# Token mixer behind adaLN linear attention on one core: fp32r sums for modulation and phi(k), u in contiguous parts, a last step cut in two

## The chip, the cores and the metric

The kernel runs on one core of a Trainium2 chip. The metric is the device time of one execution in microseconds (us). The engines of the core are named as in the profile: PE is TensorE (matmuls, with PEld for its weight loads), DVE is VectorE, ACT is ScalarE, POOL is GpSimd, and SP issues most DMAs. An engine executes its instructions in the order in which the program gives them to it, and waits where an operand is not there yet.

## The reference

Two residual blocks act on x, 2048 tokens by 448 channels, under one conditioning vector c. All values are fp32.

```python
mod = (_silu(c) @ w_mod).reshape(c.shape[0], 6, 1, -1)        # w_mod: 448 x 2688
sa, ca, ga, sb, cb, gb = (mod[:, j] for j in range(6))

h = _layernorm(x, axis=-1) * (1 + ca) + sa
q, k, v = split_heads(h @ wqkv)                               # 16 heads of 28
phi = lambda t: jnp.where(t > 0, t + 1, jnp.exp(t)) + 1e-6
pq, pk = phi(q), phi(k)
kv = einsum("bhsd,bhse->bhde", pk, v)
z = einsum("bhsd->bhd", pk)                                   # phi(k)'s sum over the tokens
o = einsum("bhqd,bhde->bhqe", pq, kv) / (einsum("bhqd,bhd->bhq", pq, z)[..., None] + 1e-6)
x = x + ga * (merge_heads(o) @ wo)

h = _layernorm(x, axis=-1) * (1 + cb) + sb
h = _layernorm(h, axis=-1)
u = gelu(einsum("bsd,sf->bdf", h, w1) + b1)                   # w1: 2048 x 1792, over the tokens
y = einsum("bdf,fs->bds", u, w2) + b2                         # w2: 1792 x 2048
x = x + gb * y.transpose(0, 2, 1)
```

## The kernel before, in words

**Arithmetic.** Most products run on TensorE in the type fp32r, and an operand that has to keep its accuracy is split into a high part, rounded to fp32r by an ACT copy, and a low part, the rest, made by a VectorE subtraction (`split`, lines 73 to 75). The product of two split operands is three matmuls: high by high, high by low, low by high (`acc3`, lines 708 to 711). Some low parts are made without VectorE: ACT writes the negated high part, and a DMA that GpSimd issues adds the full value to it in memory (`low`, lines 353 to 358; `w_low_dma`, lines 190 to 199). A few small sums use plain fp32 matmuls instead.

**Tiles.** Tokens go in 16 tiles of 128 (`NT`), the hidden dimension of the mixer in 14 tiles of 128 (`NF`). Most temporary tiles are taken from a pool of 76 slots of 2 KB per partition; a new tile waits until the earlier owner of its slot is done. The program fixes the order of the instructions by hand (`manual_schedule`).

**The stages**, in the order in which they run:

1. *Start* (lines 431 to 510). The vectors sa and ca of the modulation, then the first tiles of tokens. A modulation vector j is the sum over the 448 rows of silu(c) times a part of `w_mod`, 112 rows by 448 in each of four tiles. VectorE makes one accumulated tile of the four with the functions `mod_acc` (all at once) or `mod_part` (one tile at a time), and `mod_sum` (lines 168 to 174) adds its 112 rows with an fp32 matmul by a matrix of ones, which also spreads the result over the 128 partitions. `mod_out` copies it out of PSUM.
2. *The phi(k) loop* (lines 514 to 561), t = 3 to 15. TensorE projects k of tile t (`kp`, 11 matmuls), transposes the normalized tile t+1, and adds the outer product of tile t-3 (`a_outer`, `cacc`, 11 matmuls). VectorE and ACT make phi(k) (`a_exp` and `phi_k`, lines 321 to 329: exponential on ACT; minimum with 1 and addition of 1e-6 on VectorE; then the larger of k and 0 added on VectorE), its parts (`a_pk_parts`, lines 373 to 384), the statistics, norm and parts of the tiles ahead (`a_stats`, `a_norm_a`, `a_norm_b`, `a_high`). Phi(k) of most tiles is added to one of two running sums by a DMA of GpSimd (line 383). The vector j = 2 is made in steps 5 to 8 and summed in step 10; the parts of `w_mod` for j = 4 and 3 are loaded in steps 10 and 11.
3. *Closing the attention's sums* (lines 564 to 606). The last outer products; phi(k)'s sum `zp` over partitions by two fp32 matmuls with ones (lines 574 to 576); the vectors j = 4 and j = 3, `mod_acc` on VectorE and `mod_sum` on TensorE; the product with the v weights (`kvb`). Projections of q that were put off (`late`) fill in.
4. *The attention output and the mixer's norms* (lines 730 to 789, called stage B in this document), i = 0 to 20. Per step TensorE transposes the scaled phi(q) (`tq`), makes the attention's output of the tile before (`op`), and from step 5 on adds the product of a normalized tile and the first 512 columns of w1 (`up`). VectorE, ACT and GpSimd make the denominators (`den`, `pn`), the residual and two norms in a chain. The normalized tile's low part (`b_low2`, h2l) is made just before the next tile's scaled phi(q) (`b_scale`, pn). The vector j = 5 is added up in steps 13 to 16 and summed in step 16.
5. *First mixer product* (lines 996 to 1019): u for the other columns, only TensorE in bulk. `finish_u` applies Gelu and the factor gb, and cuts u of each hidden tile into the operands of the second product.
6. *Second mixer product* (lines 1022 to 1040). Token tiles 0 to 9 go through a scheme of seven products for each two-by-two block (`mult7`), where the moving operand is a half of u's columns (224) with its high and low part, 448 columns in all, followed by a matmul of 224 columns. Token tiles 10 to 15 are plain (`mult1`): three matmuls of all 448 columns per hidden tile. The last ten steps of the program's order are plain ones of tile 15. After the last hidden tile, VectorE adds the sum to x and SP stores the tile (`out1`, `store`).

In `finish_u` the tile `uw[f]` (4 x 224 columns) is laid out as left high, left low, right high, right low (lines 818 to 824), so that a seven product reads 448 neighbouring columns and a plain one reads two runs of 224:

```python
w4 = uw[f].rearrange("p (h x d) -> p x h d", h=2, x=2)
split(ufull[f].rearrange("p (h d) -> p h d", h=2), w4[:, 0], w4[:, 1])
```

Of the kernel before, what the change touches and what calls it, by code (L numbers as in the profile page):

```python
# [8 lines left out]
F32 = mybir.dt.float32  # L9
# [19 lines left out]
AHEAD = 8  # L29
LAG = 5  # L30
QS = {0: 2, 4: 2}
WARM = 12
# [10 lines left out]
def block_kernel(ctx: ExitStack, tc: tile.TileContext, x, wqkv, wo, w1, b1, w2, b2, c, wmod, out):  # L43
# [34 lines left out]
    ones = cst.tile([P, P], F32, name="ones")  # L78
    nc.vector.memset(ones, 1.0)
    ident = cst.tile([P, P], F32, name="ident")  # L80
    make_identity(nc, ident)
# [86 lines left out]
    def mod_sum(j, n=4):  # L168
        ps = bank(f"modp{j}")
        todo = [(scb[:, (k - 2) * P:(k - 1) * P], wm[j, k]) for k in range(n, 4)]  # L170
        todo.insert(1, (ones[:G, :], macc.pop(j)))
        for k, (a, b) in enumerate(todo):
            nc.tensor.matmul(ps[:, :D], a, b, start=(k == 0), stop=(k == len(todo) - 1))
        return ps

# [145 lines left out]
    def a_exp(t, ps):  # L321
        eks[t] = slot(f"ek{t}")
        nc.scalar.activation(eks[t], ps, AF.Exp)

    def phi_k(t, ps, new):
        dst, e = new(f"pk{t}"), eks.pop(t)
        nc.vector.tensor_scalar(e, e, 1.0, 1e-6, op0=ALU.min, op1=ALU.add)
        nc.vector.scalar_tensor_tensor(dst, ps, 0.0, e, op0=ALU.max, op1=ALU.add)
        return dst
# [145 lines left out]
    a_norm_b(2)  # L475
    w_low_dma(0, 1)
    a_stats(3)
# [36 lines left out]
    for t in range(3, NT):  # L514
# [6 lines left out]
        if t == 10:  # L521
            mp = mod_sum(2)
        if t + 1 < NT:
# [21 lines left out]
        if 5 <= t < 9:  # L545
            mod_part(2, t - 5)
        if t in (10, 11):
            load_mod(14 - t)
# [22 lines left out]
    nc.vector.tensor_add(pksum[2], pksum[2], pksum[1])  # L571
    a_q(late.pop(0))
    mod_acc(4)
    zp = bank("zp")
    for i, pk in enumerate((pksum[0], pksum[2])):
        nc.tensor.matmul(zp[:, :D], ones, pk, start=(i == 0), stop=(i == 1))
# [14 lines left out]
    split_to(6)  # L591
    mp = mod_sum(4)
    mod_acc(3)
    kvb = bank("kvb")
# [8 lines left out]
    mod_out(4, mp)  # L603
    mp = mod_sum(3)
    load_to(PRE + MID + 3)
# [125 lines left out]
    for i in range(NT + LAG):  # L731
        if i == NT - 4:
            load_mod(5)
        if NT - 3 <= i <= NT:
            mod_part(5, i - NT + 3)
        if i < NT:
            b_transpose(i)
# [5 lines left out]
        t = i - LAG  # L743
        mp = mod_sum(5) if i == NT else None
        if t >= 0:
# [58 lines left out]
    def u_parts(r, name, src):  # L804
        w = slot(f"u{name}_{r}", dt=F32R)
        split(src, w[:, :HD], w[:, HD:])
        uops[name, r] = w

    def finish_u(f, ps):
# [72 lines left out]
    def mult7(q, m):  # L882
        a, b, k, _ = PRODS[m]
        opens = m in (0, 1, 3)
        if opens:
            acc2[q, k] = bank(f"y{q}_{k}")
        ps = acc2[q, k]
        closes = m in (1, 5, 6)
        cut = hilo.pop((q, m))
        for r in range(PAIRS):  # L890
            (h, l), i = cut[r // 4], r % 4
            w = uops[b, r]
            s = slice(i * P, (i + 1) * P)
            nc.tensor.matmul(ps[:, :D], h[:, s], w, start=opens and r == 0, stop=False, skip_group_check=True)  # L894
            nc.tensor.matmul(ps[:, :HD], l[:, s], w[:, :HD], start=False, stop=closes and r == PAIRS - 1,  # L895
                             skip_group_check=True)
# [45 lines left out]
    def mult1(t, n, f):  # L942
# [3 lines left out]
        hi, lo = hilo.pop((t, n, f))  # L946
        w4 = uw[f].rearrange("p (h x d) -> p x h d", h=2, x=2)
# [74 lines left out]
    for n, (kind, p) in enumerate(order):  # L1022
# [44 lines left out]
```

## Time and profile before

| What | Before |
|---|---|
| Time, median of 3 runs | 456.86 us (456.37 to 457.12) |
| Time of the profiled execution | 457.06 us |
| Its span (first to last instruction) | 455.3 us |
| Granted TensorE clock, mean | 1.00 |
| DMA packets | 60550, 61.85 MB, mean 136 GB/s |
| phi(k) loop, projections of t = 3 to 15 | about 32.6 to 99.1 us |
| Stage B with the first 512 columns of u | about 124 to 235 us |
| First mixer product, the rest | about 235 to 323 us |
| Second mixer product | about 323 to 452 us |

The page of a profile gives for each engine its busy time, share of the span and number of instructions. Groups of instructions show line, engine, operation, output and inputs, shapes, count, then total busy time and the mean of one in ns, then the idle time of the engine before them and what ended it. The chain of waits follows the execution back from its last instruction, at each step to what released it. Matmuls overlap in a pipeline: the duration shown for one (0.36 us for 448 columns) holds its latency, and the distance between the starts of neighbours is what it costs.

### The profile page before, as it was taken

The numbers are of one execution on the slowest core, as the hardware profiler recorded it, in microseconds if no ns is written. First come the engines' busy times: TensorE is split into PE (matmuls) and PEld (weight loads), VectorE is DVE, ScalarE is ACT, GpSimd is POOL, SyncE is SP. The second block draws the span as 40 slices with busy tenths as digits, with TensorE's granted clock in tenths as the row PEclk, the third lists the DMA queues.
The fourth block names the chain that finished last, engine by engine and source line by source line (L and its number), as shares of the span: only waits on it lengthen the run. The fifth ranks groups of instructions, "written<-read, shape, count | busy, mean of one in ns | idle before, by whom it ended". The sixth has DMA issues, their size and how long they took to land.

```text
span 455.3 us, 7265 instructions
## 1 busy us (share of the span) xinstructions
PE 448.9 (99%) x2378; PEld 409.9 (90%) x2378; DVE 356.6 (78%) x781; ACT 241.7 (53%) x538; POOL 91.6 (20%) x163
## 2 busy tenths in 40 slices
PE   8999999999999999999999999999999999999996
PEld 7589998988799999988999999999999999999995
DVE  4798897887899798896559676639696977798982
ACT  1649766644466576676675445236546262535350
POOL 2124676620014355554300000000000000000000
PEclk9999999999999999999999999999999999999999
DMA  7979999994200003322307553317960583528312
GB/s 220 283 186 168 170 175 225 229 219 141 71 1 2 23 24 88 74 50 48 116 22 228 171 187 113 115 40 235 281 185 23 186 231 120 170 96 254 112 57 97
DMA packets 60550, 61.85 MB, mean 136 GB/s; under 512 B 9248, under 2 KB 53856, under 8 KB 60512
## 3 DMA queue, kind: packets, MB, share of 16 engines
q1 hardware_dynamic: 54752, 52.45, 38.5%
q0 software_dynamic: 5760, 8.95, 12.0%
q8 instruction: 18, 0.29, 0.3%
q14 instruction: 20, 0.16, 0.1%
HBM read 45.09 MB, written 7.34 MB: 115 GB/s over the span
## 4 chain that ended last, share of the span: by engine, by line
PE 80%; POOL 4%; ACT 4%; DVE 4%; DMA 3%; issue 3%; SPq 1%; POOLq 0%; DVEq 0%
PE y L894 11%; PE up L711 8%; PE up L710 8%; PE up L709 8%; PE qp L316 7%; PE y L895 6%; PE cacc L398 5%; PE kp L316 5%; PE yp L709 4%; PE yp L711 4%; PE yp L710 4%; PE op L658 4%; DMA pkl<-pk 2%; DMA wm<-in_w_mod_dram 1%; ACT y L700 1%
## 5 line engine op out<-in xcount | busy, mean ns | idle before, releaser
L711 PE MATMUL up<-h2h,pl 128*128 128x448 f32 x224 | 81.3, 363 | 0.0
L710 PE MATMUL up<-h2l,ph 128*128 128x448 f32 x224 | 81.2, 362 | 0.0
L709 PE MATMUL up<-h2h,ph 128*128 128x448 f32 x224 | 81.1, 362 | 0.0
L75 DVE TENSOR_TENSOR pl<-pr,ph 128x512 fp32r<-128x512 f32 (+1 forms) x60 | 36.4, 616 | 12.3 <-ACT ph L74 7.9
L710 PEld LDWEIGHTS up<-h2l,ph 128*128 128x128 f32 x224 | 42.1, 188 | 3.3 <-issue 0.2
L709 PEld LDWEIGHTS up<-h2h,ph 128*128 128x128 f32 x224 | 41.9, 187 | 3.1 <-issue 0.2
L711 PEld LDWEIGHTS up<-h2h,pl 128*128 128x128 f32 x224 | 42.0, 188 | 2.4
L74 ACT ACTIVATE ph<-pr 128x512 fp32r<-128x512 f32 (+1 forms) x60 | 32.8, 567 | 15.9 <-PE up L710 11.1
L900 ACT ACTIVATE cc<-y 128x448 f32<-128x448 f32 x15 | 8.2, 546 | 55.4 <-PE y L895 38.6
L709 PE MATMUL yp<-uw,qw 128*128 128x448 f32 x84 | 31.2, 371 | 0.0
L710 PE MATMUL yp<-uw,qw 128*128 128x448 f32 x84 | 30.6, 365 | 0.0
L711 PE MATMUL yp<-uw,qw 128*128 128x448 f32 x84 | 30.6, 365 | 0.0
L398 PE MATMUL cacc<-pkh,xh 128*128 128x448 f32 x64 | 24.6, 385 | 0.0
L658 PE MATMUL op<-wph,pth 112*128 112x448 f32 x64 | 24.5, 383 | 0.0
L74 ACT ACTIVATE qw<-q 128x256 fp32r<-128x256 f32 (+1 forms) x56 | 18.9, 353 | 9.0 <-DMA q<-in_B_w_dram 8.5
L398 PE MATMUL cacc<-pkl,xh 128*128 128x448 f32 x64 | 23.3, 363 | 0.2 <-DMA pkl<-pk 0.2
L658 PE MATMUL op<-wph,ptl 112*128 112x448 f32 x64 | 23.2, 362 | 0.0
L658 PE MATMUL op<-wpl,pth 112*128 112x448 f32 x64 | 23.2, 362 | 0.0
L316 PE MATMUL kp<-wh,hh 128*128 128x448 f32 x60 | 22.0, 371 | 0.0
L316 PE MATMUL qp<-wh,hh 128*128 128x448 f32 x60 | 21.9, 371 | 0.0
L75 DVE TENSOR_TENSOR qw<-q,qw 128x256 fp32r<-128x256 f32 (+1 forms) x56 | 18.9, 352 | 3.8 <-ACT qw L74 3.8
L316 PE MATMUL kp<-wh,hl 128*128 128x448 f32 x60 | 21.7, 366 | 0.1
(198 smaller groups left out, 1221.0 us busy)
## 6 DMA issues: line engine op xcount, KB each, us to landing
pr<-in_B_w_dram SPq DMA_DIRECT2D x48, 256.0 KB, 3.0
a<-in_B_w_dram SPq DMA_DIRECT2D x20, 256.0 KB, 5.0
wm<-in_w_mod_dram SPq DMA_DIRECT2D x24, 196.0 KB, 5.0
a<-in_B_w_dram SPq DMA_DIRECT2D x20, 192.0 KB, 4.9
x<-in_A_x_dram SPq DMA_DIRECT2D x16, 224.0 KB, 4.6
xpark<-x SPq DMA_DIRECT2D x16, 224.0 KB, 1.9
q<-in_B_w_dram SPq DMA_DIRECT2D x28, 128.0 KB, 3.3
xb<-xpark SPq DMA_DIRECT2D x16, 224.0 KB, 4.1
```

The costliest lines, as they stand in the source:

```text
L74: nc.scalar.activation(hi, full, AF.Copy)
L75: nc.vector.tensor_sub(lo, full, hi.bitcast(F32))
L316: nc.tensor.matmul(o, a[:, ch * P:(ch + 1) * P], b, start=(n == 0), stop=(n == 10))
L398: nc.tensor.matmul(cacc[ch][:, :D], a[:, s], b, start=(t == 0 and i == 0), stop=(t == NT - 1 and i == len(todo) - 1))
L658: nc.tensor.matmul(opb[t][:, :D], a[:, s], b, start=(n == 0), stop=(n == 11))
L700: nc.scalar.activation(ys[t], ys[t], AF.Identity, bias=nb, scale=rs)
L709: nc.tensor.matmul(ps[:, :D], hi[:, sl], mh, start=first, stop=False)
L710: nc.tensor.matmul(ps[:, :D], hi[:, sl], ml, start=False, stop=False)
L711: nc.tensor.matmul(ps[:, :D], lo[:, sl], mh, start=False, stop=last)
L894: nc.tensor.matmul(ps[:, :D], h[:, s], w, start=opens and r == 0, stop=False, skip_group_check=True)
L895: nc.tensor.matmul(ps[:, :HD], l[:, s], w[:, :HD], start=False, stop=closes and r == PAIRS - 1, skip_group_check=True)
L900: nc.scalar.activation(cop[q, name], acc2[q, k][:, :D], AF.Copy)
```

## The change

It has seven parts.

1. *Modulation vectors j = 2 to 5*: the accumulated tile is split (`mod_split`) and summed by two fp32r matmuls with a matrix of ones in fp32r (`mod_sum2`) instead of one fp32 matmul. Vectors 0 and 1 stay as they are.
2. *Additions for j = 4 and j = 3*: one tile of `w_mod` at a time, in steps 11 to 14 (j = 4) and, two and two, in step 15 and just after the loop (j = 3), instead of `mod_acc` in the stage after the loop.
3. *phi(k)'s sum*: both running sums are added on VectorE, the result is split and summed by two fp32r matmuls, now behind the last outer product.
4. *phi(k)*: ACT also makes a Relu of k, and VectorE does one operation, min(exp, 1) + Relu, instead of two. The constant 1e-6 is added while the parts are made, and to z when `zb` is copied (2048 times 1e-6).
5. The low part of one q weight tile (`w_low(0, 1)`) by VectorE instead of ACT and GpSimd's DMA; and in stage B `b_scale` ahead of `b_low2`.
6. *u in contiguous parts*: `uw[f]` holds all 448 high columns, then all 448 low columns. A plain product reads one run of 448; the seven products that read u itself (b11, b21, b22) read two runs of 224. The operands of the other four (t1 to t4) stay contiguous.
7. *The last three hidden tiles of token tile 15*: the sum so far is closed and added to x; the nine remaining matmuls are done for columns 0 to 335, then for columns 336 to 447, each with its own PSUM bank, addition and store.

```diff
+LAST, CUT = 3, 336
+MOD_AT = {11: [(4, 0)], 12: [(4, 1)], 13: [(4, 2)], 14: [(4, 3)], 15: [(3, 0), (3, 1)]}
...
+    ones_r = cst.tile([P, P], F32R, name="ones_r")
+    nc.scalar.activation(ones_r, ones, AF.Copy)
...
+    def mod_split(j):
+        acc = macc.pop(j)
+        macc[j] = (moving(slot, f"mh{j}", parts=G), moving(slot, f"ml{j}", parts=G))
+        split(acc, *macc[j])
+
+    def mod_sum2(j):
+        ps = bank(f"modp{j}")
+        hi, lo = macc.pop(j)
+        nc.tensor.matmul(ps[:, :D], ones_r[:G, :], hi, start=True, stop=False)
+        nc.tensor.matmul(ps[:, :D], ones_r[:G, :], lo, start=False, stop=True)
         return ps
...
     def a_exp(t, ps):
-        eks[t] = slot(f"ek{t}")
-        nc.scalar.activation(eks[t], ps, AF.Exp)
+        eks[t] = (slot(f"ek{t}"), slot(f"rk{t}"))
+        nc.scalar.activation(eks[t][0], ps, AF.Exp)
+        nc.scalar.activation(eks[t][1], ps, AF.Relu)
+
     def phi_k(t, ps, new):
-        dst, e = new(f"pk{t}"), eks.pop(t)
-        nc.vector.tensor_scalar(e, e, 1.0, 1e-6, op0=ALU.min, op1=ALU.add)
-        nc.vector.scalar_tensor_tensor(dst, ps, 0.0, e, op0=ALU.max, op1=ALU.add)
+        dst, (e, r) = new(f"pk{t}"), eks.pop(t)
+        nc.vector.scalar_tensor_tensor(dst, e, 1.0, r, op0=ALU.min, op1=ALU.add)
         return dst
...
-        nc.scalar.activation(hi, pk, AF.Copy)
-        low(t, lo, pk, hi)
+        nc.scalar.activation(hi, pk, AF.Copy, bias=1e-6)
+        if t in DVE_LOW:
+            nc.vector.scalar_tensor_tensor(lo, pk, 1e-6, hi.bitcast(F32), op0=ALU.add, op1=ALU.subtract)
+        else:
+            nc.scalar.activation(lo, hi.bitcast(F32), AF.Copy, scale=-1.0, bias=1e-6)
+            nc.gpsimd.dma_start(lo, pk, accum_op=ALU.add)
...
-    w_low_dma(0, 1)
+    w_low(0, 1)
...
         if t == 10:
-            mp = mod_sum(2)
+            mp = mod_sum2(2)
...
+        if t == 9:
+            mod_split(2)
+        for j, i in MOD_AT.get(t, ()):
+            mod_part(j, i)
...
+    for i in (2, 3):
+        mod_part(3, i)
     split_to(2)
     nc.vector.tensor_add(pksum[2], pksum[2], pksum14[0])
     nc.vector.tensor_add(pksum[2], pksum[2], pksum[1])
     a_q(late.pop(0))
-    mod_acc(4)
+    nc.vector.tensor_add(pksum[2], pksum[2], pksum[0])
+    zs = (moving(slot, "zh"), moving(slot, "zl"))
+    split(pksum[2], *zs)
+    a_outer(NT - 1)
     zp = bank("zp")
-    for i, pk in enumerate((pksum[0], pksum[2])):
-        nc.tensor.matmul(zp[:, :D], ones, pk, start=(i == 0), stop=(i == 1))
-    a_outer(NT - 1)
+    for i, pk in enumerate(zs):
+        nc.tensor.matmul(zp[:, :D], ones_r, pk, start=(i == 0), stop=(i == 1))
+    mod_split(4)
+    mod_split(3)
     load_to(14)
     split_to(4)
     zb = tslot("zb")
-    nc.scalar.activation(zb, zp[:, :D], AF.Copy)
+    nc.scalar.activation(zb, zp[:, :D], AF.Copy, bias=S * 1e-6)
...
-    mp = mod_sum(4)
-    mod_acc(3)
+    mp = mod_sum2(4)
...
-    mp = mod_sum(3)
+    mp = mod_sum2(3)
...
+        if i == NT:
+            mod_split(5)
...
-        mp = mod_sum(5) if i == NT else None
+        mp = mod_sum2(5) if i == NT else None
...
+        if scale:
+            b_scale(i + 1)
         if norm2:
             b_low2(i - 4)
-        if scale:
-            b_scale(i + 1)
...
-            w4 = uw[f].rearrange("p (h x d) -> p x h d", h=2, x=2)
-            split(ufull[f].rearrange("p (h d) -> p h d", h=2), w4[:, 0], w4[:, 1])
+            split(ufull[f], uw[f][:, :D], uw[f][:, D:])
+            w = uw[f].rearrange("p (x d) -> p x d", x=2)
+            left, right = ((w[:, :, h:h + HD], w[:, 0, h:h + HD]) for h in (0, HD))
             if f % 2:
-                uops["b21", r], uops["b22", r] = uw[f][:, :D], uw[f][:, D:]
+                uops["b21", r], uops["b22", r] = left, right
             else:
-                uops["b11", r] = uw[f][:, :D]
+                uops["b11", r] = left
...
-            acc3(acc2[t + i], hi, lo, slice(i * P, (i + 1) * P), w4[:, 0], w4[:, 1], f == 0, f == NF - 1)
+            acc3(acc2[t + i], hi, lo, slice(i * P, (i + 1) * P), uw[f][:, :D], uw[f][:, D:], f == 0,
+                 f == NF - 1 - (LAST if t == NT - 1 else 0))
+
+    def mult_last(t):
+        nc.vector.tensor_add(X[t], acc2[t][:, :D], X[t])
+        for c0, c1 in ((0, CUT), (CUT, D)):
+            ps = bank(f"yl{c0}")[:, :c1 - c0]
+            n = 0
+            for f in range(NF - LAST, NF):
+                wh, wl = hilo[t, 1, f]
+                a, b = uw[f][:, c0:c1], uw[f][:, D + c0:D + c1]
+                for w, m in ((wh, a), (wh, b), (wl, a)):
+                    nc.tensor.matmul(ps, w, m, start=n == 0, stop=n == 3 * LAST - 1)
+                    n += 1
+            x = X[t][:, c0:c1]
+            nc.vector.tensor_add(x, ps, x)
+            nc.sync.dma_start(of[t * P:(t + 1) * P, c0:c1], x)
...
-        (mult7 if kind == "s" else mult1)(*p)
-        (out7 if kind == "s" else out1)(*p)
+        if n < len(order) - LAST:
+            (mult7 if kind == "s" else mult1)(*p)
+            (out7 if kind == "s" else out1)(*p)
+    mult_last(NT - 1)
```

More of the change, by code (lines that the diff above doesn't have):

```diff
@@ L173, in mod_sum @@
             nc.tensor.matmul(ps[:, :D], a, b, start=(k == 0), stop=(k == len(todo) - 1))
+        return ps
+    def mod_split(j):
[7 more added lines that the diff above has]
+        nc.tensor.matmul(ps[:, :D], ones_r[:G, :], lo, start=False, stop=True)
         return ps
@@ L806, in u_parts @@
         split(src, w[:, :HD], w[:, HD:])
-        uops[name, r] = w
+        uops[name, r] = (w, w[:, :HD])
     def finish_u(f, ps):
@@ L891, in mult7 @@
             (h, l), i = cut[r // 4], r % 4
-            w = uops[b, r]
+            w, wh = uops[b, r]
             s = slice(i * P, (i + 1) * P)
             nc.tensor.matmul(ps[:, :D], h[:, s], w, start=opens and r == 0, stop=False, skip_group_check=True)
-            nc.tensor.matmul(ps[:, :HD], l[:, s], w[:, :HD], start=False, stop=closes and r == PAIRS - 1,
+            nc.tensor.matmul(ps[:, :HD], l[:, s], wh, start=False, stop=closes and r == PAIRS - 1,
                              skip_group_check=True)
@@ L946, in mult1 @@
         hi, lo = hilo.pop((t, n, f))
-        w4 = uw[f].rearrange("p (h x d) -> p x h d", h=2, x=2)
         for i in range(n):
-            acc3(acc2[t + i], hi, lo, slice(i * P, (i + 1) * P), w4[:, 0], w4[:, 1], f == 0, f == NF - 1)
+            acc3(acc2[t + i], hi, lo, slice(i * P, (i + 1) * P), uw[f][:, :D], uw[f][:, D:], f == 0,
[14 more added lines that the diff above has]
+            nc.sync.dma_start(of[t * P:(t + 1) * P, c0:c1], x)
     def out1(t, n, f):
```

## The prediction

> **What bounds the kernel now.** The page of the profile comes first: the engines' busy time and, further down, the shares of the chain that ended last.
>
> ```profile
> PE 448.9 (99%) x2378; PEld 409.9 (90%) x2378; DVE 356.6 (78%) x781; ACT 241.7 (53%) x538; POOL 91.6 (20%) x163
> ...
> PE 80%; POOL 4%; ACT 4%; DVE 4%; DMA 3%; issue 3%; SPq 1%; POOLq 0%; DVEq 0%
> ```
>
> TensorE works from end to end. Its busy figure overlaps neighbouring matmuls, so I price a matmul by the distance between starts. The chain of waits in order of time (start, duration, what) gives such distances; these rows surround the edits.
>
> ```profile
> 92.34 2.08 PE kp L316 x9
> ...
> 105.87 2.20 PE qp L316 x11
> 108.07 1.50 PE zp L576 x4
> 109.57 2.21 PE cacc L398 x11
> 111.79 2.21 PE qp L316 x11
> 113.99 0.75 PE modp L173 x2
> 114.75 3.15 PE kvb L598 x32
> 117.89 0.77 PE modp L173 x2
> ...
> 214.64 0.75 PE modp L173 x2
> ```
>
> An fp32r matmul of 448 columns takes 2.20/11 = 0.200 us; an fp32 one counts as two instructions and takes 1.50/2 = 0.75 us. From 105.87 to 118.66 the chain is TensorE's without a gap. In two stretches it also runs through other engines: around 64 to 92 us, in the phi(k) loop, and 159 to 207 us, in what I call stage B. The timeline (start, duration, engine, line, tiles, wait) shows what TensorE lost there.
>
> ```profile
> 74.18 0.47 PE L398 MATMUL cacc<-pkl,xh 128*128 128x448 f32 x1 [0.24 <-DMA pkl<-pk]
> 195.09 0.37 PE L711 MATMUL up<-h2h,pl 128*128 128x448 f32 x1
> 195.84 0.62 PE L642 MATMUL tq<-ident,pn 128*112 128x128 f32 x4 [0.38 <-DVE pn L631]
> 206.19 0.37 PE L711 MATMUL up<-h2h,pl 128*128 128x448 f32 x1
> 206.78 0.62 PE L642 MATMUL tq<-ident,pn 128*112 128x128 f32 x4 [0.23 <-DVE pn L631]
> ```
>
> The next start is due 0.20 after a matmul's; 195.09 to 195.84 is 0.75 and 206.19 to 206.78 is 0.59, so TensorE lost 0.55 + 0.39 = 0.94 us waiting for pn. The rest is nearly a sum of matmuls, and the change is priced as that sum.
>
> **zp, phi(k)'s sum.** Two fp32 matmuls (1.50) become two fp32r ones (0.40): **-1.10 us**. Their operand must be split first: three additions of VectorE instead of two, an ACT copy and a subtraction now precede zp. It is also moved behind the last outer product (2.21), so it starts near 105.87 + 2.20 + 2.21 = 110.28. In the old trace the second addition starts at 105.48:
>
> ```profile
> 105.48 0.62 DVE L571 TENSOR_TENSOR pk<-pk,pk 128x448 f32<-128x448 f32 x1
> ```
>
> Four such steps end near 107.9, 2.4 us ahead of zp; without that cover, what exceeds it is a stall. ACT's copy zb now comes near 110.9 and the two copies of cacc queue behind it, so all three end by about 112.5 at 0.54 each (L334 below); kvb, which waits for them, starts at 110.68 + 2.20 + 0.40 = 113.3. Covered, by 0.8 us.
>
> **The modulation vectors j = 2 to 5.** For j = 4, 3 and 5 the sums go from 0.75 + 0.77 + 0.75 to 3 x 0.40: **-1.07 us**. The eight additions for j = 4 and 3 leave VectorE between 106 and 117 us and go to steps 11 to 15 of the phi(k) loop and just behind it. SP had issued w_mod's part 4 long before:
>
> ```profile
> 65.15 2.18 SPq L107 DMA_DIRECT2D wm<-in_w_mod_dram  x4
> ```
>
> Step 11 ends near 88 (below), 20 us later, and part 3 has a similar lead, so I charge no wait for a DMA. For j = 5 a split now stands between the last addition and the matmul:
>
> ```profile
> 211.69 0.63 ACT L226 ACTIVATE pl<-ph 128x512 fp32r<-128x512 f32 x1
> ```
>
> ACT is free at 212.3; a copy and a subtraction of some 0.6 each end near 213.5, the matmul starts at 214.64: hidden by 1.1 us, or by 0.4 if TensorE gains 0.74 on ACT before (below). Behind the waiting subtraction VectorE queues the residual of the next tile, and GpSimd waits for its sum to make the mean. If the cover goes, up to 0.5 is lost.
>
> **The phi(k) loop.** Per step VectorE loses L327 (a minimum and an addition in one), ACT gains a Relu like L334, and steps 11 to 14 gain one addition like L166 (mean ns behind the busy time):
>
> ```profile
> L334 ACT ACTIVATE rq<-qp 128x448 f32<-128x448 f32 x16 | 8.7, 541 | 0.0
> L327 DVE TENSOR_SCALAR ek<-ek 128x448 f32<-128x448 f32 x16 | 6.2, 386 | 1.5 <-ACT ek L323 1.5
> L905 DVE TENSOR_TENSOR xb<-xb,cc 128x224 f32<-128x224 f32 x15 | 5.9, 392 | 0.5
> L166 DVE SCALAR_TENSOR_TENSOR acc<-wm,sc,acc 112x448 f32<-112x448 f32 x6 | 4.1, 679 | 0.0
> ```
>
> Before step 11 VectorE's 0.39 a step is worth nothing where TensorE bounds, and ACT, half busy, has room for 0.54. In steps 11 to 14 VectorE has 0.68 - 0.39 = 0.29 more. Step 11 hides it, step 12 does not:
>
> ```profile
> 87.96 0.69 DVE L283 SCALAR_TENSOR_TENSOR h<-h,rs,mod 128x448 f32<-128x448 f32 x1 [0.44 <-POOL rs L272]
> 91.60 0.68 DVE L75 TENSOR_TENSOR hl<-tp,hh 128x512 fp32r<-128x512 f32 x1
> ```
>
> VectorE idles 0.44 for GpSimd's rs before 87.96, then runs to hl, which ends at 92.28; TensorE's kp goes on at 92.34. So the 0.35 that j = 2 wins at step 10 is waited away here, and VectorE's 0.29 may be added; and the Relu delays ACT's pkl copy, whose DMA came just in time at 74.18. Bounds: -0.35 (all kept) to +0.8 (0.29 and one Relu of 0.54). I take **0.0** for this part, j = 2 included, since the rows show another chain level with TensorE there. One w_low moves from ACT and GpSimd's queue to VectorE, 0.62 against the 0.39 dropped beside it: nothing. The constant ones_r is made at the start, where ACT waits for c.
>
> **b_scale ahead of b_low2.** pn, which ended the stalls, stood behind the subtraction h2l:
>
> ```profile
> 194.10 0.24 DVE L627 RECIPROCAL den<-den 128x16 f32<-128x16 f32 x1
> 194.53 0.62 DVE L706 TENSOR_TENSOR h2l<-y,h2h 128x448 fp32r<-128x448 f32 x1 [0.19 <-ACT h2h L703]
> 195.08 0.62 DVE L631 SCALAR_TENSOR_TENSOR pn<-pq,den 128x448 f32<-128x448 f32 x1
> ```
>
> It can start at 194.34 instead of 195.08, 0.74 earlier. The two stalls add up to a lag of 0.94, of which this takes 0.74: **-0.74 us** (0 to -0.94). h2l, late by one instruction, is used in the next step, 5.5 us on (195.84 to 206.78 are two steps).
>
> **u in contiguous parts.** Before, a plain step's moving operand is two runs of 224 columns and a seven's one of 448; after, plain steps have one run, and three of the seven products (b11, b21, b22) have two. Starts of matmuls, first stage (contiguous) and plain (two runs):
>
> ```profile
> 249.84 0.36 PE L711 MATMUL up<-h2h,pl 128*128 128x448 f32 x1
> 253.44 0.36 PE L711 MATMUL up<-h2h,pl 128*128 128x448 f32 x1
> ...
> 444.80 0.36 PE L709 MATMUL yp<-uw,qw 128*128 128x448 f32 x1
> 451.33 0.37 PE L711 MATMUL yp<-uw,qw 128*128 128x448 f32 x1
> ```
>
> 18 distances in 3.60 make 0.200; 32 in 6.53 make 0.204. Two runs cost 4 ns. Plain steps: 252 matmuls x 4 ns = -1.01. Sevens: 3 x 35 wide matmuls x 4 ns = +0.42, being the same shape of access; 0 if the narrow matmuls between hide it, 0.84 at twice that. **-0.6 us** (-1.0 to -0.2).
>
> **The last steps in 336 and 112 columns.** What follows the last matmul, which starts at 451.33:
>
> ```profile
> 451.73 0.62 DVE L955 TENSOR_TENSOR xb<-yp,xb 128x448 f32<-128x448 f32 x1 [2.55 <-PE yp L711]
> 452.39 0.34 SPq L909 DMA_DIRECT2D out_dram<-xb  x1
> ```
>
> The last nine matmuls start at 451.33 - 8 x 0.204 = 449.70. Nine of 336 columns at 0.15 end at 451.06. Nine of 112 take 0.05 each in proportion, or 0.098 as in kvb (3.15/32), the row nearest in width, which I take: the last starts at 451.84, its sum is ready 0.25 later, and the add takes 0.28 (0.62 and 0.39 for 448 and 224 columns, continued), so the store is issued near 452.4, as now. The first store, near 451.85, is off SP by then; the partial sum's addition to x falls under the 336 columns. **0.0 us**, with -0.4 at the proportional pace and +0.5 if a store of 448-byte rows lands late. The Trainium skill, "TensorE: Matmul & The Clock Gate", LDWEIGHTS, says that a weight load takes as long as its columns need at 1.2 GHz, whatever streams behind it: an estimate of 107 ns for 128 columns, by which the end comes 0.1 later than mine; kvb's 98 ns with 112 columns of weights agrees (93 by the rule). The Trainium skill, "DMA: Bandwidth & Descriptors", Specifications, also says that pieces under 512 B are read, modified and written; no row here shows such a store.
>
> **Sum** against the profiled execution (457.06, its span and 1.8 around it): -1.10 - 1.07 + 0.0 - 0.74 - 0.6 + 0.0 = -3.5, so 453.55. That execution stood 0.2 over the median of 456.86: **453.4 us**. Some 0.2%, 0.9 us, is what tells a change from none here.
>
> **Rivals.** *Stage B takes it back.* VectorE, ACT and GpSimd are close to TensorE there (window; PE, weight loads, VectorE, ACT, GpSimd, clock, DMA):
>
> ```profile
> 160.00:180.00 20.00, 20.00 (x109) 18.59 (x108) 19.20 (x47) 14.50 (x32) 10.47 (x21) 1.00 0.13 39
> ```
>
> VectorE is busy 19.20 of 20. If that loop keeps its own time, the 1.82 won before it (zp, j = 4 and 3) returns as waits for pn: 456.86 - 3.5 + 1.8 = 455.2. Against it: the loop starts from TensorE's transposes, and eight additions leave VectorE just before. *More of everything*: j = 2 kept, both stalls gone, sevens unpenalised, the tail at proportional pace: 453.4 - 0.35 - 0.2 - 0.4 - 0.4 = 452.0. *Slower*: the Relu sits on ACT ahead of the copies pkh and pkl, GpSimd issues their DMAs in order, and each outer product waits for pkl. Once that chain is longer than TensorE's step, each step from 7 to 14 pays a Relu: 8 x 0.54 = 4.3, so 457.7. It decides from the point where pkl's margin, none at 74.18, is under 0.54 in all these steps; that TensorE waited for pkl once speaks against it. *The edits don't pay*: waits for the low halves replace the fp32 passes at zp and the vectors, and the rest cancels: 456.7.
>
> **Chances.** Forecast 0.62 (452.4 to 454.6), more of everything 0.12, stage B takes it back 0.12, no pay 0.05, slower 0.09. 452.0 to 455.8 leaves out the last two and an edge of the outer ones, under 0.2. Faster by over 0.2%: 0.84; within: 0.07, the unpaying case and an edge of stage B's; slower: 0.09.
>
> **What would show it.** zp and four modp of two instructions at 0.40 on the chain, each followed at once by the next matmul; no wait of tq for pn; plain distances of 0.200, sevens on uw up to 4 ns a matmul longer; the last nine matmuls about 0.1 apart. I am wrong if outer products or kp wait more for pkl or hl than now, if waits of tq or of the j = 5 sum take the gain, or if the last store lands late.

## The result, and the profile after

The changed kernel takes 452.63 us (median of 6 runs, 452.36 to 453.98) where the kernel before takes 456.99 us (6 runs, 456.28 to 457.24): a ratio of 0.9908, interval 0.9888 to 0.9927. The forecast was 453.4 us. The profiled execution of the changed kernel took 452.57 us with a span of 450.8 us, against 457.06 and 455.3, so the two traces stand for the medians and differ by 4.6 us of span where the sum of the prediction had 3.5. Two of the six runs of the changed kernel stand at 453.97 and 453.98; no profile shows such a run, so the reason is open.

The page of the changed kernel, engines' busy time and shares of the chain:

```profile
PE 446.0 (99%) x2385; PEld 411.0 (91%) x2385; DVE 356.0 (79%) x774; ACT 250.1 (55%) x559; POOL 89.0 (20%) x162
...
PE 92%; POOL 3%; issue 3%; DVE 1%; ACT 0%; POOLq 0%; DVEq 0%
```

TensorE has more of the chain, 92% for 80%: the waits in the phi(k) loop and in stage B, where the chain left it, are mostly gone. What TensorE still waits for (engine, line, releaser: total us, times, longest):

```profile
PE warm L141 <- DVE mhalf L95: 1.1, 1, 1.1
PE kp L333 <- DVE hl L77: 0.6, 1, 0.6
PE tp L437 <- DVE h L432: 0.2, 1, 0.2
```

No wait for pkl, the low part of phi(k), and none for pn is left in this list. One wait for hl, the low part of the normalized tile, is longer than before, in the loop. The chain of the changed kernel around the sums (start, duration, what):

```profile
91.43 2.07 PE kp L333 x9
...
107.15 2.20 PE cacc L420 x11
109.35 0.41 PE zp L607 x2
109.76 2.20 PE qp L333 x11
112.37 3.15 PE kvb L629 x32
...
208.78 2.42 PE op L689 x12
```

zp is two instructions in 0.41 us, and the projections follow at once. To see where the 4.6 us come from, the starts of the same instructions in both traces:

| Start of | Before | After | Shift | Gain since the row above |
|---|---|---|---|---|
| first kp | 15.36 | 15.03 | -0.33 | -0.33 |
| outer product of tile 7 | 73.49 | 73.03 | -0.46 | -0.13 |
| outer product of tile 8 | 79.61 | 78.29 | -1.32 | -0.86 |
| outer product of tile 11 | 94.61 | 93.70 | -0.91 | +0.41 |
| kvb | 114.58 | 112.20 | -2.38 | -1.47 |
| first wp | 120.70 | 117.98 | -2.72 | -0.34 |
| tq of tile 12 | 190.03 | 187.31 | -2.72 | 0 |
| tq of tile 15 | 206.78 | 203.34 | -3.44 | -0.72 |
| first yp | 323.24 | 319.46 | -3.78 | -0.34 |
| last nine matmuls | 449.70 | 445.46 | -4.24 | -0.46 |
| end | 455.34 | 450.77 | -4.57 | -0.33 |

Here wp is the first product with the output weights, and yp a plain step of the second mixer product. The rows from kvb to the first yp are the sums of zp, j = 4, 3 and 5 and, between tq of tile 12 and of tile 15, the swap in stage B. Three parts had no value in the prediction's sum: the start, the loop (the three rows after it) and the tail. They make 0.33 + 0.58 + 0.33 = 1.24 of the 4.57 us.

### The profile page after: what moved, and what is told of

The parts are those of the page before. It is cut to its first block, busy times and chain, and to the rows that moved or that the text cites. A ratio compares the mean times of both kernels' runs of the same rounds, so it can differ in the third digit from the quotient of the medians.

```text
span 450.8 us, 7295 instructions
## 1 busy us (share of the span) xinstructions
PE 446.0 (99%) x2385; PEld 411.0 (91%) x2385; DVE 356.0 (79%) x774; ACT 250.1 (55%) x559; POOL 89.0 (20%) x162
## 4 chain that ended last, share of the span: by engine, by line
PE 92%; POOL 3%; issue 3%; DVE 1%; ACT 0%; POOLq 0%; DVEq 0%
PE y L928 11%; PE up L742 10%; PE up L741 10%; PE up L740 10%; PE op L689 9%; PE qp L333 7%; PE y L929 6%; PE kp L333 4%; PE cacc L420 4%; PE yp L740 4%; PE yp L742 4%; PE yp L741 4%; PE warm L141 2%; PE tq L673 2%; POOL rs L289 1%
## 5 line engine op out<-in xcount | busy, mean ns | idle before, releaser
L740 PE MATMUL yp<-uw,qw 128*128 128x448 f32 x81 | 29.8, 367 | 0.0
L742 PE MATMUL yp<-uw,qw 128*128 128x448 f32 x81 | 29.4, 363 | 0.0
L741 PE MATMUL yp<-uw,qw 128*128 128x448 f32 x81 | 29.4, 363 | 0.0
```

The source lines that it names most:

```text
L740: nc.tensor.matmul(ps[:, :D], hi[:, sl], mh, start=first, stop=False)
L741: nc.tensor.matmul(ps[:, :D], hi[:, sl], ml, start=False, stop=False)
L742: nc.tensor.matmul(ps[:, :D], lo[:, sl], mh, start=False, stop=last)
```

## The experiments

Each ratio is to the kernel before as it ran beside that experiment (medians of 456.66 to 456.98 us).

**The swap of b_scale and b_low2 alone**, on the kernel before:

```diff
+        if scale:
+            b_scale(i + 1)
         if norm2:
             b_low2(i - 4)
-        if scale:
-            b_scale(i + 1)
```

> The kernel before with one edit: b_scale ahead of b_low2. Theory (pn stood behind h2l, and TensorE lost 0.94 us waiting for it): about 0.7 us less than before, 456.2 by the medians; the waits of tq for pn fall from two of together 0.94 us to one under 0.3 us, nothing else moves. Rival (stage B keeps its own time, set by ACT and GpSimd): no gain, the same two waits. If the changed kernel's smaller waits came from its other edits, this run also shows no gain.

Measured: 456.04 us (11 runs) against 456.98 us (23 runs), ratio 0.9984 (0.9973 to 0.9994). In its trace everything up to tq of tile 12 keeps about the same distance from the trace of before (0.29 to 0.37 us, 0.31 of it there at the first kp), and between tq of tile 12 and of tile 15 it gains 0.71 us more. No wait for pn is listed any more; a stall of 0.26 us is left ahead of tq of tile 15, as in the changed kernel. The gain of 0.72 in the changed kernel is the swap's.

**u's layout alone**, on the kernel before: `uw[f]` as 448 high and 448 low columns, b11, b21 and b22 with two runs.

```diff
-            w4 = uw[f].rearrange("p (h x d) -> p x h d", h=2, x=2)
-            split(ufull[f].rearrange("p (h d) -> p h d", h=2), w4[:, 0], w4[:, 1])
+            split(ufull[f], uw[f][:, :D], uw[f][:, D:])
```

> The kernel before with u's parts contiguous and nothing else. Theory (a moving operand in two runs costs 4 ns a matmul): 0.5 us less than before, 456.4 by the medians; three plain matmuls in 0.600 us instead of 0.613, a seven on uw 0.012 us longer than before, a seven on t1 to t4 unchanged. Rival (the gain in the changed kernel comes from tiles that lie elsewhere in memory, since the constant ones_r shifts them by 512 bytes): plain steps stay at 0.613 or the sevens change as well.

Measured: 456.31 us (12 runs), ratio 0.9986 (0.9972 to 1.0): by the times alone hardly told from nothing. The trace tells more, since this stage is TensorE's alone: from the first yp to the last matmul it gains 0.49 us, as the changed kernel does up to its last nine (0.46). Added up over all distances between starts, in this run the plain matmuls gain 0.57 us, the sevens on u itself lose 0.18, and those on t1 to t4 gain 0.11. Only the long runs of plain matmuls, the first 48 and the last 36, go from 0.204 to 0.200 us. The groups of six between sevens go from about 0.204 to 0.203. The rival of the moved tiles does not fit, since the plain steps did change, and the sevens on t1 to t4 by only 0.4 ns a matmul of 448 columns.

**The last step whole**, and **cut elsewhere**, on the changed kernel. The first leaves `mult_last` out; the second is

```diff
-LAST, CUT = 3, 336
+LAST, CUT = 2, 224
```

> The changed kernel with the last step of token tile 15 whole again (448 columns, one add, one store). Theory A (the narrow last store lands sooner: 1.19 us after its issue in the changed kernel against 1.60 for a whole tile before): 0.3 us more than the changed kernel, 452.9; the last nine matmuls end 0.3 us sooner, the add takes 0.62 us, the store lands 1.6 us after its issue. Theory B (the shorter last add is what the cut brings, 0.27 against 0.62 us): the store lands after the same 1.2 us here, and the kernel is not slower, about 452.4. The order of columns and sums is otherwise the same.

> The changed kernel with only the last two hidden tiles cut, in 224 and 224 columns. Theory (matmuls of 224 columns at 0.11 us waste less than those of 112 at 0.104; the last add takes 0.39 instead of 0.27): the last store is issued 0.2 us sooner counted from the same matmul; if a store of 896-byte rows lands as soon as one of 448 (1.2 us after its issue), 452.4; if it lands like a whole tile (1.6), 452.8. Which of the two it is tells whether the width of the rows or the size of the store makes the landing shorter.

Measured: whole 452.69 us (4 runs), ratio 0.9906 (0.9892 to 0.992); 2 steps at 224 columns 452.51 us (5 runs), ratio 0.9901 (0.9879 to 0.9922). The times don't tell the three apart; the traces do. After the last step, whole:

```profile
447.00 0.37 PE L742 MATMUL yp<-uw,qw 128*128 128x448 f32 x1
447.40 0.62 DVE L990 TENSOR_TENSOR xb<-yp,xb 128x448 f32<-128x448 f32 x1 [2.44 <-PE yp L742]
448.06 0.34 SPq L943 DMA_DIRECT2D out_dram<-xb  x1
```

The changed kernel, 336 and 112 columns:

```profile
440.26 0.36 PE L741 MATMUL yp<-uw,qw 128*128 128x448 f32 x1
...
445.06 0.36 PE L741 MATMUL yp<-uw,qw 128*128 128x448 f32 x1
...
445.46 2.48 PE L995 MATMUL yl<-uw,qw 128*128 128x336 f32 x18
...
447.57 1.05 SPq L999 DMA_DIRECT2D out_dram<-xb  x2
447.98 0.27 DVE L998 TENSOR_TENSOR xb<-yl,xb 128x112 f32<-128x112 f32 x1 [0.44 <-PE yl L995]
```

And 2 steps at 224 columns:

```profile
445.26 1.49 PE L995 MATMUL yl<-uw,qw 128*128 128x224 f32 x12
446.61 0.94 SPq L999 DMA_DIRECT2D out_dram<-xb  x2
446.79 0.39 DVE L998 TENSOR_TENSOR xb<-yl,xb 128x224 f32<-128x224 f32 x1 [0.21 <-PE yl L995]
```

The row of two issues ends with the second, and an issue lasts 0.34, so the last store is issued at 447.57 + 1.05 - 0.34 = 448.28 with 112 columns and at 446.61 + 0.94 - 0.34 = 447.21 with 224. From there to the ends of the spans (450.77 and 449.84) it is 2.49 and 2.63 us; with the whole store it is 451.02 - 448.06 = 2.96. The smaller last store ends sooner, by up to 0.47 us, and that is where the cut gains: its issue comes 2.82 us after the start of the last nine matmuls, where before it came 2.69 after (452.39 - 449.70). From the start of the last nine matmuls to the end of the span it is 450.77 - 445.46 = 5.31 us with the cut and 451.02 - 445.40 = 5.62 without, so the cut is worth 0.31 us.

**phi(k) as before**, on the changed kernel:

```diff
-        nc.scalar.activation(eks[t][1], ps, AF.Relu)
...
-        nc.vector.scalar_tensor_tensor(dst, e, 1.0, r, op0=ALU.min, op1=ALU.add)
+        nc.vector.tensor_scalar(e, e, 1.0, 1e-6, op0=ALU.min, op1=ALU.add)
+        nc.vector.scalar_tensor_tensor(dst, ps, 0.0, e, op0=ALU.max, op1=ALU.add)
```

> The changed kernel with phi(k) made as before (no Relu on ACT, the minimum and the larger-of as two operations of VectorE). Theory A (the change of phi(k) did nothing for TensorE in steps 3 to 10, and gave VectorE 0.39 us a step where VectorE bounds, in steps 11 to 14): the wait of kp for hl near 91 us grows from 0.7 us to 1.1 us or more, the rest is as in the changed kernel, 453 by the median. Theory B (the Relu on ACT was a cost, for it delays pkl): the outer products wait less and the kernel is faster, 452.2. Theory C (the operation taken away held the memory port that GpSimd needs, and its going is what removed the wait for pkl of 0.5 us at outer product 7): that wait returns.

**A second Relu in every step**, into the same tile, on the changed kernel:

```diff
         nc.scalar.activation(eks[t][1], ps, AF.Relu)
+        nc.scalar.activation(eks[t][1], ps, AF.Relu)
```

> The changed kernel with the Relu of phi(k) made twice in each step, an extra 0.43 to 0.54 us of ACT a step. It measures the cover of ACT's work in the loop. If ACT has room (the changed kernel's ACT is about two thirds busy there): within 0.3 us of the changed kernel, 452.6 to 452.9. If the loop's chain over ACT, GpSimd's DMAs and pkl has no more margin: each step from 4 on pays, up to 4 us, 456.

Measured: with the old phi(k) 454.14 us (6 runs), ratio 0.9938 (0.992 to 0.9957); with two Relus 453.15 us (6 runs), ratio 0.9914 (0.9896 to 0.9932). In the changed kernel the new phi(k) is worth 1.5 us by the medians; the traces agree, since with the old one TensorE takes 1.60 us longer from the first kp to kvb. These 1.60 us lie mainly at two kinds of places. 0.68 are lost by the outer product of tile 1, in two stalls of 0.34 where kp waits for hl (kp starts at 25.47 and 39.92 us). The kernel before, which has the old phi(k) too, loses only 0.14 there; the difference of 0.54 most likely comes from the low part of the q weight tile, which only the other kernel's VectorE makes, ahead of the first of these hl. So the 1.5 us are not all a gain over the kernel before. And 0.94 are lost at outer products that wait for pkl: 0.58 at tile 9 and 0.36 at tile 10. Theories A and B are refuted: the wait for hl near 92 us does not grow (0.47 against 0.57 by the bracket), and the kernel is not faster. The wait that theory C expected is there, at other tiles; the cause that it names was not tested.

A second Relu costs half a microsecond in all (0.52 by the medians, 0.44 by the traces up to kvb), far from 0.54 in each of eight steps. It shows at three places: 0.40 are lost ahead of the outer product of tile 1, where a transpose waits for ACT, and 0.47 at the outer product of tile 9, which waits for pkl; 0.42 come back at hl.

The wait at tile 9, two tiles later than the one of the kernel before:

```profile
83.71 0.45 PE L416 MATMUL cacc<-pkh,xh 128*128 128x448 f32 x1
84.48 0.47 PE L416 MATMUL cacc<-pkl,xh 128*128 128x448 f32 x1 [0.32 <-DMA pkl<-pk]
```

The next start is due 0.29 after the first of an outer product (88.01 to 88.30 in the changed kernel), so 0.77 means 0.48 lost. The DMA that makes this pkl (GpSimd issues it) and the loads of w_mod beside it (SP issues them), first with the old phi(k), then in the changed kernel:

```profile
77.56 1.23 POOL L376 DMA_DIRECT2D pkl<-pk  x1
76.63 2.19 SPq L111 DMA_DIRECT2D wm<-in_w_mod_dram  x4
```

```profile
77.30 0.86 POOL L399 DMA_DIRECT2D pkl<-pk  x1 [0.26 <-issue]
75.31 4.88 SPq L111 DMA_DIRECT2D wm<-in_w_mod_dram  x4
```

The issue is only 0.26 us earlier in the changed kernel, but the DMA lands 5.4 us after it, where with the old phi(k) it takes 6.9. The same holds for tile 7, for which the kernel before waited, first before (its loads of w_mod, 65.15 and 2.18 long, are shown in the prediction), then after:

```profile
66.58 0.86 POOL L358 DMA_DIRECT2D pkl<-pk  x1 [0.29 <-issue]
```

```profile
66.56 0.87 POOL L399 DMA_DIRECT2D pkl<-pk  x1 [0.74 <-ACT pkl L398]
66.23 4.99 SPq L111 DMA_DIRECT2D wm<-in_w_mod_dram  x4
```

From the first kp on, this issue is even later in the changed kernel (51.53 against 51.22 us), but the DMA lands after 5.9 us and not after 7.6. So the wait went because the DMA lands sooner, not because it starts sooner. In all six traces with the old phi(k) the four loads of w_mod near it are issued within 1.4 to 2.2 us and it takes 7.0 to 7.6 us; in all seven with the Relu they are spread over 3.9 to 4.9 us and it takes 5.5 to 6.2. That the loads beside it slow it is likely, but no run moved them alone. Nor is it shown what spreads them: a load waits for a free slot of the pool, and the new phi(k) both takes an operation from VectorE and takes one slot more in each step.

**The fp32r sums without the moved additions**, in two forms: on the kernel before, sums alone (j = 2 to 5 and zp, phi(k) old):

```diff
     a_outer(NT - 1)
+    zp = bank("zp")
+    for i, pk in enumerate(zs):
+        nc.tensor.matmul(zp[:, :D], ones_r, pk, start=(i == 0), stop=(i == 1))
+    mod_acc(4)
+    mod_split(4)
...
-    mp = mod_sum(4)
+    mp = mod_sum2(4)
     mod_acc(3)
+    mod_split(3)
```

> The kernel before with fp32r sums for j = 2 to 5 and for zp (split operands), the additions of w_mod for j = 4 and 3 left behind the loop, phi(k) as before. Theory (the sums are matmul time, and the splits are covered): zp 1.1, four vectors 0.35 each, together 2.5 us less than before, 454.4, if j = 2 is kept; 2.1 less if the loop waits it away. Rival (with all additions behind the loop VectorE comes too late): TensorE waits for the low half of j = 4 ahead of kvb by 1 us or more, and the gain is about 1 us.

and on the changed kernel, the additions of j = 4 and 3 back behind the loop, all else kept:

```diff
-MOD_AT = {11: [(4, 0)], 12: [(4, 1)], 13: [(4, 2)], 14: [(4, 3)], 15: [(3, 0), (3, 1)]}
+MOD_AT = {}
...
+    mod_acc(4)
     mod_split(4)
-    mod_split(3)
...
     mp = mod_sum2(4)
+    mod_acc(3)
+    mod_split(3)
```

> The changed kernel with the additions of w_mod for j = 4 and 3 behind the phi(k) loop again. Theory A (an addition in steps 11 and 12 is what makes TensorE wait 0.7 us for hl instead of 0.3, and behind the loop VectorE had cover): 0.4 us less than the changed kernel, 452.2, no wait ahead of kvb. Theory B (behind the loop there is no cover, the splits come late): the wait for hl is 0.3 us or none, but TensorE waits at j = 4 or kvb, and the kernel is 0.5 to 2 us slower than the changed one.

Measured: sums alone 460.51 us (6 runs), ratio 1.0081 (1.0058 to 1.0104): slower than before. Additions back 457.73 us (12 runs), ratio 1.0018 (0.9999 to 1.0037): 5.1 us slower than the changed kernel, all of its gain; its runs lie far apart (455.72 to 460.66), and in the traces the difference is 4.7 us from the first kp to the end. TensorE in the second of them:

```profile
111.12 3.40 PE L629 MATMUL kvb<-cs,wr 128*112 128x112 f32 x32
117.48 0.47 PE L189 MATMUL modp<-mh,ones_r 112*128 112x448 f32 x1 [2.96 <-ACT mh L76]
118.14 0.47 PE L190 MATMUL modp<-ml,ones_r 112*128 112x448 f32 x1 [0.19 <-DVE ml L77]
118.45 0.53 PE L333 MATMUL qp<-wh,hh 128*128 128x448 f32 x1
...
122.24 3.17 PE L754 MATMUL wp<-wo,kvm 112*112 112x448 f32 x8
```

and its VectorE, the last additions of j = 3:

```profile
114.63 2.13 DVE L162 SCALAR_TENSOR_TENSOR acc<-wm,sc,acc 112x448 f32<-112x448 f32 x3
```

The trace of before has for the same three:

```profile
115.10 2.13 DVE L158 SCALAR_TENSOR_TENSOR acc<-wm,sc,acc 112x448 f32<-112x448 f32 x3
```

There they end at 117.23, and the sum follows kvb at 114.58 + 3.15 = 117.73: ready by 0.5. With the shorter sums, no waits in the loop and a start 0.69 us earlier, TensorE is at kvb 3.46 us earlier (111.12), VectorE's additions only 0.47, since VectorE now also makes the splits of phi(k)'s sum and of the vectors and waits 0.70 us for ACT's high part in each. The last addition ends at 116.76, the two parts follow it, and TensorE waits for them. TensorE idles 2.96 us, and after that the eleven projections from 118.45 to 122.24 take 3.79 us and not 2.20. The windows of this trace show the granted clock at 0.64 behind the gap:

```profile
111.00:117.40 6.40, 3.52 (x33) 3.22 (x32) 5.34 (x10) 2.95 (x8) 0.00 (x0) 1.00 0.40 125
117.40:122.20 4.80, 4.54 (x13) 3.84 (x14) 4.14 (x7) 2.36 (x6) 0.23 (x1) 0.64 0.01 2
```

**The gap filled.** The kernel with the additions back, and 12 matmuls whose result is overwritten, ahead of the sum of j = 3:

```diff
     def mod_sum2(j):
         ps = bank(f"modp{j}")
+        for _ in range(12 if j == 3 else 0):
+            nc.tensor.matmul(ps[:, :P], ones, ones, start=True, stop=True)
```

> The kernel with the additions back behind the loop (457.7 us), and 12 more fp32 matmuls of 128 columns, into the bank that the sum of part 3 then overwrites, ahead of that sum: TensorE has work in place of the 2.96 us of idle time. Theory: the idle time costs 3.0 us, and the lower granted clock behind it (0.64 from 117.4 to 122.2 us) another 1.8 us; with the gap filled the clock stays at 1.00 and the time falls to about 455.9 us, though the wait for the split stays. Rival: the lower clock does not come from the gap; then it stays at 457.7 us or rises by what the matmuls overrun.

Measured: 455.95 us (12 runs), ratio 0.9981 (0.9969 to 0.9994): 1.8 us below the kernel with the gap by the medians, though the split comes no sooner. The windows of its trace:

```profile
111.00:117.40 6.40, 6.40 (x59) 6.09 (x58) 5.80 (x10) 2.96 (x8) 0.00 (x0) 1.00 0.39 119
117.40:122.20 4.80, 4.34 (x19) 3.15 (x18) 4.00 (x7) 2.96 (x7) 0.00 (x0) 1.00 0.03 10
```

The clock stays at 1.00, and from kvb to the first wp this kernel takes 1.59 us less, which is 3.79 - 2.20. With the additions behind the loop, the way from kvb to the first wp is 5.35 us longer than in the changed kernel: 2.96 of waiting, 1.59 of slow projections, and the rest at the sum itself, whose low half is late too. 0.83 us come back at hl, which no addition delays there.

**The additions alone**, sums in fp32, on the kernel before:

```diff
+        for j, i in {11: [(4, 0)], 12: [(4, 1)], 13: [(4, 2)], 14: [(4, 3)], 15: [(3, 0), (3, 1)]}.get(t, ()):
+            mod_part(j, i)
...
+    for i in (2, 3):
+        mod_part(3, i)
...
-    mod_acc(4)
...
-    mod_acc(3)
```

> The kernel before, sums still in fp32, with only the additions of parts 4 and 3 of w_mod moved into steps 11 to 15 of the loop and ahead of phi(k)'s sum. Theory A: the additions matter only as a cover for the fp32r sums; with fp32 sums the kernel before waited 0.5 us for acc at 117.7 us, so at most that is gained, and step 12's addition in front of hl takes 0.4 us back: 456.9 us, range 456.2 to 457.3. Theory B: the additions are worth the 5 us that the changed kernel lost without them, whatever the sums do: 452 us.

Measured: 457.51 us (11 runs) against 456.66 us (23 runs), ratio 1.0014 (1.0005 to 1.0022): slower by 0.85 us by the medians (0.6 by the ratio), a little beyond the upper end that theory A gave. Theory B is refuted. A's sum held a mistake of its own: the 0.5 us wait for acc in the trace of before is not at 117.7 us (there the sum follows kvb at once, as worked out above) but at the first vector's sum, at 9.62 us, so there was nothing to gain; the time from kvb to the first wp is 6.12 us in both. What remains is the loss in the loop, where the step between the outer products of tiles 10 and 11 grows by 0.76 us, from 5.28, with a wait of 0.9 us for hl. Moved additions without fp32r sums lose, fp32r sums without moved additions lose, both together gain.

**The addition out of step 12**, and the cut of 2 steps at 224 columns, on the changed kernel:

```diff
-LAST, CUT = 3, 336
-MOD_AT = {11: [(4, 0)], 12: [(4, 1)], 13: [(4, 2)], 14: [(4, 3)], 15: [(3, 0), (3, 1)]}
+LAST, CUT = 2, 224
+MOD_AT = {11: [(4, 0)], 13: [(4, 1)], 14: [(4, 2), (4, 3)], 15: [(3, 0), (3, 1)]}
```

> The changed kernel with the one addition that stood in step 12 of the phi(k) loop put into step 13, step 13's into step 14 (two there), and the last steps of u cut as 2 steps at 224 columns. Theory: the 0.57 us that TensorE waits for hl at 91 us in the changed kernel comes from that one addition standing ahead of hl on VectorE; without it the wait falls to 0.1 us or nothing, step outer10 to outer11 falls from 5.7 to about 4.9 us, and nothing comes back later, since VectorE idles 1.23 us in step 14. Expected 452.6 - 0.75 (wait) - 0.1 (cut) = 451.8 us, range 451.3 to 452.3. Rival: the wait only moves to the hl of step 14 or to the splits behind the loop: 452.4 to 452.7 us.

Measured: 451.68 us (4 runs, 451.45 to 452.44), ratio 0.9893 (0.9879 to 0.9908). The fastest of all, though its interval overlaps that of the changed kernel. VectorE in the changed kernel, then in this one:

```profile
89.56 0.68 DVE L170 SCALAR_TENSOR_TENSOR acc<-wm,sc,acc 112x448 f32<-112x448 f32 x1
90.16 0.62 DVE L586 TENSOR_TENSOR wo<-wo,mod 112x448 f32<-112x448 f32 x1
90.69 0.69 DVE L77 TENSOR_TENSOR hl<-tp,hh 128x512 fp32r<-128x512 f32 x1
```

```profile
89.16 0.62 DVE L586 TENSOR_TENSOR wo<-wo,mod 112x448 f32<-112x448 f32 x1
89.70 0.68 DVE L77 TENSOR_TENSOR hl<-tp,hh 128x512 fp32r<-128x512 f32 x1
90.30 0.68 DVE L294 SCALAR_TENSOR_TENSOR h<-x,mv,mod 128x448 f32<-128x448 f32 x1
```

The addition is gone from in front of hl, the wait for hl falls from 0.57 to 0.15, and the step between the outer products of tiles 10 and 11 from 5.69 to 5.29. The expected 4.9 is not reached; the kernel with all additions behind the loop has 4.86. What separates 5.29 from 4.86 was not tried; the addition in step 11, the only one left ahead of this place, is a candidate, though VectorE idles 0.47 us for GpSimd between it and this place. Of the 1.1 us by which this span is shorter, 0.60 are there at the first kp already, so the edit's own part is 0.39 in the loop and 0.14 at the end.

## Why the prediction held, step by step

*zp* (-1.10): right in size, and covered as forecast, if by less. The gain from the outer product of tile 11 to kvb is 1.47: 1.12 from zp and 0.35 from j = 4. The split of phi(k)'s sum ends at 107.83 in the trace (forecast 107.9), zp starts at 109.19: 1.4 us of cover where the prediction had 2.4, since TensorE arrives sooner.

*j = 4, 3 and 5* (-1.07): measured 0.35 + 0.34 + 0.34. No wait at any of them. But a part of the change that the prediction left without a price carries them: it named that eight additions leave VectorE, and gave that no value of its own. Without it the kernel is 5.1 us slower, because TensorE then runs ahead of VectorE's queue and a gap of 2.96 us lowers the clock. The rival *the edits don't pay* described that place, at 456.7; with the additions back it came to 457.7. That the additions were in the change and not in the sum is luck, as far as the prediction goes.

*b_scale* (-0.74): measured -0.72, and -0.71 alone. Of the stall of 0.39 ahead of tq of tile 15, 0.26 is left:

```profile
202.88 0.37 PE L742 MATMUL up<-h2h,pl 128*128 128x448 f32 x1
203.34 0.62 PE L673 MATMUL tq<-ident,pn 128*112 128x128 f32 x4
```

The rival *stage B takes it back* fell: the shift is 2.72 us at the first wp and at tq of tile 12.

*u* (-0.6): measured -0.46, and -0.49 alone. Plain steps run at 0.200 (24 distances in 4.80 us between the two starts shown), as forecast. But only their long runs gain 4 ns a matmul; by the run of u alone the plain ones bring 0.57 together and not 1.01, and the sevens on u give back 0.18 and not 0.42. Each was forecast at about twice its size; that the difference came out near the forecast is in part luck, since the two errors work against each other.

*The phi(k) loop* (0.0, from -0.35 to +0.8): this is the term that was mis-sized. From the first kp to the outer product of tile 11 the changed kernel gains 0.58. The step that it got wrong reads "VectorE's 0.39 a step is worth nothing where TensorE bounds". At hl it had a price of 0.13 near 40 us. And with the new phi(k) the wait for the DMA of pkl went: 0.24 by the bracket that the prediction quoted, it had cost 0.51, the gain of 0.86 at tile 8 less the 0.35 of j = 2. The prediction named this wait and gave its going no value. It went because the DMA landed 1.6 us sooner beside more widely spread loads of w_mod; which part of the new phi(k) spreads them stays open, so these 0.51 us are shown to belong to it but not to VectorE's time. The pair of w_low and the dropped operation was rightly priced at nothing; with the old phi(k), w_low most likely costs the 0.54 told above. The rest went much as the prediction wrote: j = 2's 0.35 is won at step 10, and at hl, where step 12's addition stands in front, 0.41 is lost again; the prediction had 0.35 lost there and perhaps 0.29 more. The rival *slower* had the Relu as the cause of a wait in each step from 7 to 14; even with two Relus one outer product waits so, and the cost is 0.5 us in all.

*The tail* (0.0, from -0.4 to +0.5): measured -0.33. The matmuls went as priced: by the distances between starts 0.153 for 336 columns against 0.15, and 0.104 for 112 against 0.098 (0.112 without the first, and 0.111 for 224 columns in the other cut). The Trainium skill, "TensorE: Matmul & The Clock Gate", LDWEIGHTS, makes it an estimate of 107 ns; the trace lies nearer to that than to 98. What failed is the assumption that a store lands as late whatever its size. The Trainium skill, "DMA: Bandwidth & Descriptors", Specifications, says that pieces under 512 B are read, modified and written; the store of 448-byte rows was nonetheless over sooner, 2.49 us from issue to the end of the span against 2.96 for whole rows.

*The start* (not priced): 0.33 of the difference of the two traces. The first kp starts between 14.38 and 15.36 us in the thirteen profiled executions, and that of the kernel before is the latest of them. It is not put down to the change.

## What to carry to other kernels

When an edit shortens the engine that bounds, look at which engine makes its operands a few steps on, and by how much they were early: here it was 0.5 us for the last vector, less than the edits ahead of it won, and the same additions moved 11 to 22 us earlier were the condition of the whole gain. A transfer that arrives just in time is a price that the sum has to hold: ask what its going would be worth, and what else is loaded beside it. When such a wait goes, compare its issue and its landing separately before naming the cause. Move work of an engine that has time to spare by one place only after reading what stands next in the queue: one addition in front of hl cost 0.4 us, and a step later it cost nothing that the trace shows.

## What the runs showed of the hardware

- A gap of 2.96 us on TensorE was followed by a granted clock of 0.50: eleven matmuls of 448 columns took 3.79 us for 2.20. It held some 3.4 us in one trace (118.5 to 121.9) and nearly 7 us in that of the sums alone, which has such a gap too (118.7 to 125.5). It does not come each time: of the twelve runs with the additions back the fastest, 455.72 us, has a mean clock of 1.000, the others 0.991 to 0.996. Gaps of under 1 us, as at hl, left the clock at 1.00. The Trainium skill, "TensorE: Matmul & The Clock Gate", Part 1, gives one idle window of about 3.4 us as the condition for half the clock; here less than 3 us of idle time were enough.
- Matmuls with nothing to compute, put into the gap, kept the clock at 1.00 and were worth 1.8 us.
- A DMA of GpSimd that adds a tile of phi(k) took 7.0 to 7.6 us from issue to landing where four loads of w_mod were issued within 1.4 to 2.2 us around it, and 5.5 to 6.2 where they were spread over 3.9 to 4.9. The thirteen traces fall into these two groups; no run moved the loads alone.
- With 128 columns of weights, fp32r matmuls of 224 and of 112 columns start 0.111 and 0.112 us apart, those of 336 and 448 columns 0.153 and 0.200.
- From the issue of the last store to the end of the span: 2.96 us for rows of 448 columns, 2.63 for 224, 2.49 for 112.
